# RWKV attention and an eight-expert MoE on one core: chunk loads cut into even and odd rows, two GpSimd products swapped, two weight loads moved by some steps

## The chip, the core and the metric

The kernel runs on one NeuronCore of a Trainium2 chip. The metric is device time in microseconds (us) of one launch. The kernel before has three timed runs of 278.13, 279.83 and 283.46 us; their median, 279.83 us, is what the changed kernel is held against.

## The reference

Two stages in float32. Attention, for 4 batches, 8 heads, 768 tokens and 48 channels a head, is a linear recurrence:

```
for t in range(S):
    y[t]  = r[t] @ (state + outer(u * k[t], v[t]))
    state = w[t][:, None] * state + outer(k[t], v[t])
```

The MoE takes the 3072 rows of 384 channels that come out: a row is computed only where `x @ w_skip > 0`; its expert is the argmax of `x @ w_gate` over 8; then `x + p * (relu(x @ w1[e]) @ w2[e])` with p the softmax weight of that expert. Other rows pass through.

## The kernel before, in words

**Attention.** The sequence is cut into 24 chunks of 128 tokens (6 for each batch, lines 56 to 58). A chunk lies on 128 partitions, two groups of four heads, as one tile `wrk` with three column ranges: w (up to `R_OFF`), r (up to `K_OFF`) and k (up to `V_OFF`). Three `wrk` buffers rotate, so chunk i + 3 can be loaded once GpSimd has read chunk i for the last time. For a chunk, VectorE runs two scans over w: `q` (line 308) and, after a small reciprocal (line 323), `rh` (line 330). GpSimd forms three products of 128 x 512: `rk` = r k (line 317, needs the chunk alone), `kq` = k q (line 325, needs the scan `q`) and `rp` = r rh (line 334, needs the scan `rh`). TensorE multiplies `kq` and `rp` into `psA` (scores, line 358), `rk` into `psY` (line 377), transposes `kq` (line 348), and after VectorE has masked `psA` (line 364, two halves `asb`) and scaled `psY` (line 381) it forms the outputs (lines 409 and 413), which ScalarE copies out as `xT` (line 418) and which are turned back on TensorE (line 425), copied by ScalarE and stored.

**Order of the work.** It is written out by hand: a loop over steps s from -2 to 24. Step s prepares chunk s + 2 (scans on VectorE, products on GpSimd), scores chunk s + 1, finishes chunk s and stores chunk s - 1. Each engine runs its own instructions in this order. SyncE (SP) issues nearly all DMAs, also in this order: the load of chunk s + 4, the turned v `vt` (two DMAs, line 157) and v (line 177) of chunk s + 3, the store of chunk s - 1 (line 435), and in some steps one third of a weight tile (line 86, 512 KB). In the compiled program an SP DMA also waits until the SP DMA eight places before it has landed, since they share eight semaphores in turn.

**Weights.** `load_weights(e, q)` brings 1.5 MB, the w1 (q = 0) or w2 (q = 1) of expert e, in three thirds, one a step. Steps 5 to 7 load w2 of expert 0 into buffer r1; steps 16 to 18 load w1 of expert 1 into the same buffer, steps 19 to 21 load w1 of expert 0 into r0. The w2 of expert 0 is split into a high and a low part as it lies in r1 (ScalarE line 108, GpSimd line 109, one slice a step); the first slice of expert 1's w1 is split from step 18 on.

**Router.** After chunks 10, 18 and 24 a generator `router` is advanced between the attention's instructions. It marks token places: `hot` (on GpSimd line 538, on ScalarE lines 541 and 542, on VectorE line 536), and it splits gate weights: `gds` and `vals` on GpSimd (lines 582 and 586), `factors` on ScalarE (line 595), which VectorE reads behind the next scan `q`.

**MoE.** From the last step on TensorE runs the experts back to back: line 135 (w1 of expert 0 straight from r0), 671, then 901 to 903 and 927 to 929 for the experts 1 to 7. Rows are gathered and scattered by GpSimd's indirect DMAs (lines 446, 622, 838).

Of the kernel before, what the change touches and what calls it, by code (L numbers as in the profile page):

```python
# [43 lines left out]
V_OFF = K_OFF + NP * P  # L44
# [13 lines left out]
def rwkv_moe_kernel(ctx, tc, wrk, wrk0, vN, uP, wgs, wgp, w12, cst, out):  # L58
    nc = tc.nc
# [59 lines left out]
    def drain(g):  # L119
        for _ in g:  # L120
            pass
# [20 lines left out]
    with tc.tile_pool(name="att", bufs=2) as att, \  # L142
# [7 lines left out]
        def half(g, n_=HP):  # L150
            return slice(HP * g, HP * g + n_)
# [7 lines left out]
        def load_turned(i):  # L159
            for o in range(2):  # L160
                load_vt(nc.sync, vt_sb[i % (NBUF + 1)], i, o)

        cuts = {i: ((0, R_OFF), (R_OFF, V_OFF)) for i in range(5)}

        def load_chunk(i):
            b, c = seq[i]
            rows = wrk.rearrange("b c g d n -> (b c g d) n")
            at = 2 * D * chunk[i]
            t = wrk_sb[i % NBUF]
            to, at = (t, at - KO) if 0 < chunk[i] < n - 1 else (t[KO:LO], at)  # L170
            for c0, c1 in cuts.get(i, ((0, V_OFF),)):
                yield nc.sync.dma_start(to[:, c0:c1], rows[at:at + to.shape[0], c0:c1])

        def load_v(i):
            b, c = seq[i]
            v_sb[i] = att.tile([P, H, D], F32, tag="v", name=f"v{i}", bufs=4)
            nc.sync.dma_start(v_sb[i], vN[b, c])
# [114 lines left out]
        def mark_some(k=2):  # L292
            for _ in range(min(k, len(marks))):
                marks.popleft()()
# [5 lines left out]
        def prep_scan(i):  # L300
            wk = work[i] = {}
            t = wrk_sb[i % NBUF]
            n_ = NP * CW
            a3 = lambda z: z.rearrange("p (a j) -> p a j", a=NP)
            wk["w"] = t
            wk["r"], wk["k"] = a3(t[:, R_OFF:K_OFF]), a3(t[:, K_OFF:V_OFF])
            q = wk["q"] = att.tile([P, NP, CW], F32, tag="q", name=f"q{i}", bufs=2)
            nc.vector.tensor_tensor_scan(  # L308
                q.rearrange("p a j -> p (a j)")[:, ::-1], t[:, 1:1 + n_][:, ::-1],
                ones_at[:, 1:1 + n_][:, ::-1], 0.0, op0=ALU.mult, op1=ALU.max)  # L310
            rk = wk["rk"] = att.tile([P, NP, P], F32, tag="rk", name=f"rk{i}")
            if i > 1:
                bonus_keys(i)

        def bonus_keys(i):
            t = wrk_sb[i % NBUF]
            nc.gpsimd.tensor_tensor(work[i]["rk"].rearrange("p a j -> p (a j)"),  # L317
                                    t[:, R_OFF:K_OFF], t[:, K_OFF:V_OFF], op=ALU.mult)

        def prep_keys(i):  # L320
            wk = work[i]
            heads = wk["w"][:, 0:NP * CW].rearrange("p (a j) -> p a j", a=NP)
            nc.vector.reciprocal(heads[:, :, 0:1], wk["q"][:, :, 0:1])
            kq = wk["kq"] = att.tile([P, NP, P], F32, tag="kq", name=f"kq{i}")
            nc.gpsimd.tensor_tensor(kq, wk["k"], wk["q"][:, :, 1:1 + P], op=ALU.mult)  # L325

        def prep_reads(i):
            wk = work[i]
            rh = wk["rh"] = att.tile([P, NP, CW], F32, tag="rh", name=f"rh{i}", bufs=2)
            nc.vector.tensor_tensor_scan(  # L330
                rh.rearrange("p a j -> p (a j)"), wk["w"][:, 0:NP * CW], reads_at[:, :NP * CW],
                rowsk, op0=ALU.mult, op1=ALU.max)
            rp = wk["rp"] = att.tile([P, NP, P], F32, tag="rp", name=f"rp{i}", bufs=3)
            nc.gpsimd.tensor_tensor(rp, wk["r"], rh[:, :, :P], op=ALU.mult)  # L334
            if i < 2:
                bonus_keys(i)
# [339 lines left out]
        def fill(k, w=512):  # L676
            psw = ps1.tile([P, 512], F32, tag="psT", name="psw", bufs=2)
            for _ in range(k):
                nc.tensor.matmul(psw[:, :w], warm[:, :P], warm[:, :w], start=True, stop=True)

        with tc.manual_schedule():
            setup()
            fill(FILL0)
            parts = [(4, 0, i) for i in range(6, 12)] + [(15, 1, 0)] + [(19, 1, i) for i in range(1, 6)]
            for s in range(-2, n + 1):
                on = lambda i: 0 <= i < n
                if s == -2:
                    z = wgp[half(0), :2]
                    z = bass.AP(z.tensor, z.offset,
                                [z.ap[0], [(HP * NP + 2) * XW, 2], [1, 2 * XW]])  # L690
                    nc.sync.dma_start(wgp_sb[half(0)].rearrange("p g s x -> p g (s x)"), z)
                    for g in range(2):
                        at = 2 * (g ^ 1)
                        nc.sync.dma_start(wgp_sb[half(1), g, :, 2 * D:],
                                          wgp[half(g), at:at + 2, 2 * D:])
                if 3 <= s + 4 < n:
                    chunk_parts = load_chunk(s + 4)
                    if s + 4 in cuts:
                        next(chunk_parts)
                        load_v(s + 2)  # L700
                    drain(chunk_parts)
                if on(s + 3) and s + 3 >= 1:
                    load_turned(s + 3)
                    if s + 5 not in cuts:
                        load_v(s + 3)
                if s == 1:
                    nc.sync.dma_start(c_sb[:, C_IOTA:], cst[:, C_IOTA:])
                if s == LATE:
                    nc.sync.dma_start(wgs_sb, wgs)
                if on(s - 1):  # L710
                    store(s - 1)
                marked = len(marks)
                if pace[0] == 1:
                    mark_some()
                for i0, m in GROUPS:
                    if i0 + m == s:
                        pace[0] = 1 if i0 + m < LATE else 2
                        later.append(router(i0, m))
                        if i0 + m == LATE:
                            later.append(early())  # L720
                if on(s):
                    update(s)
                if on(s + 2):
                    prep_scan(s + 2)
                drip(pace[0])
                if on(s):
                    outputs(s)
                if on(s + 2):
                    prep_keys(s + 2)
                    drip(pace[0])  # L730
                    prep_reads(s + 2)
                while low_parts:
                    low_parts.pop()()
                if on(s):
                    evict(s)
                    carry(s)
                if on(s + 1):
                    scores(s + 1)
                    bonus_sums(s + 1)
                    rows_of_keys(s + 1)  # L740
                    if s == -1:
                        fill(2)
                        fill(3, 8)
                    flush()
                    mask(s + 1, 0)
                    mask(s + 1, 1)
                    bonus(s + 1)
                    drip(3 * pace[0])
                if on(s + 2):
                    prep_check(s + 2)  # L750
                if s == n - 1:
                    early_tokens(0)
                if on(s):
                    rows_out(s)
                flush(False)
                if pace[0] > 1:
                    mark_some(4)
                if s in (1, 2, 3):
                    nc.scalar.copy(*((trib, tri), (identb, ident),
                                     (iota, c_sb[:, C_IOTA:C_IOTA + 2 * P]))[s - 1])  # L760
                if s == 4:
                    nc.scalar.copy(desc[:, 0], c_sb[:, C_DESC:C_DESC + E])
                    nc.scalar.copy(toks_ps[:, :GROUPS[-1][1], :, 0], tok[:, GROUPS[-1][0]:])
                k = s + 1 - W_AT
                for eq, k0 in (((0, 1), 2), ((1, 0), 13), ((0, 0), 16)):
                    if k == k0:
                        gens[eq] = load_weights(*eq)
                    if k0 <= k < k0 + 3:
                        next(gens[eq])
                for _ in range(1 if s < 22 else 2):  # L770
                    if parts and k >= parts[0][0] and (not marked or s == 15):
                        split_high(*parts.pop(0)[1:])
# [346 lines left out]
```

## Time and profile before

| what | value |
|---|---|
| median of three runs | 279.83 us |
| the profiled execution: its time, and its span from first to last instruction | 279.76 us, 277.9 us |
| TensorE busy | 264.4 us (95%) |
| VectorE busy | 211.9 us (76%) |
| ScalarE, GpSimd busy | 157.1 us (57%), 146.6 us (53%) |
| DMA | 64.33 MB, mean 231 GB/s |
| attention, from the first scores to the first expert's matmul | 7.6 to 131.6 us |

Busy shares are means over unlike stages: the attention uses all engines and the DMA queues, the MoE mostly TensorE. A row of the timeline begins with start and duration in us; what stands in brackets is the idle time of the engine just before the row and what ended it.

### The profile page before, as it was taken

To read this page: it belongs to the slowest core of one execution; us is meant where nothing else is said; L and a number is where in the kernel's file an instruction comes from. 1 tells how busy PE (TensorE), PEld (TensorE's weight loads), DVE (VectorE), ACT (ScalarE), POOL (GpSimd) and SP (SyncE) were. 2 spreads that over 40 slices of the span, in tenths; PEclk is the share of its full clock that TensorE was granted. 3 is DMA by queue.
4 is the path that set the end of the run, shared out by engine and by line. 5 is a ranking of instruction groups with operands and counts; after the bars stand their busy time and mean duration, and the time that the engine had idled before them with its cause. 6 is when DMAs were issued, how large, how long until landed. Compare 5 with 4: busy or idle time off the path is not lost.

```text
span 277.9 us, 8937 instructions
## 1 busy us (share of the span) xinstructions
PE 264.4 (95%) x3599; PEld 244.0 (88%) x3600; DVE 211.9 (76%) x396; ACT 157.1 (57%) x456; POOL 146.6 (53%) x141
## 2 busy tenths in 40 slices
PE   8899799998999999899999999999999999999992
PEld 3688688887888888787999999999999999999992
DVE  7989789999999999972748597957859488594310
ACT  4365556775788857767326482926729276391300
POOL 6888677798999997984656636011030110201111
PEclk9999999999999999999999999999999999999998
DMA  7999999999877999961078997765662656700001
GB/s 244 279 300 326 322 331 366 374 333 312 270 229 253 319 351 344 267 233 61 28 227 302 337 310 255 240 229 225 225 248 81 235 212 226 266 14 28 9 5 42
DMA packets 26402, 64.33 MB, mean 231 GB/s; under 512 B 4062, under 2 KB 15380, under 8 KB 26352
## 3 DMA queue, kind: packets, MB, share of 16 engines
q1 hardware_dynamic: 24176, 58.37, 63.2%
q0 software_dynamic: 2048, 5.30, 6.0%
q8 instruction: 30, 0.49, 0.7%
q14 instruction: 20, 0.16, 0.2%
q10 hardware_dynamic: 128, 0.00, 0.0%
HBM read 56.61 MB, written 7.67 MB: 231 GB/s over the span
## 4 chain that ended last, share of the span: by engine, by line
PE 71%; DMA 8%; issue 6%; DVE 5%; POOL 4%; ACT 4%; SPq 0%; POOLq 0%; DVEq 0%
PE psO L927 7%; PE psO L929 7%; PE psO L928 6%; PE psH L901 6%; PE psH L902 6%; PE psH L903 6%; PE psY L409 6%; DMA wrk<-wrk 5%; PE psH L135 4%; PE psX L425 4%; PE psA L358 4%; PE psY L413 3%; PE psT L348 3%; PE psY L377 2%; DMA r<-w 2%
## 5 line engine op out<-in xcount | busy, mean ns | idle before, releaser
L838 POOL DMA_INDIRECT out<-fin,ids x16 | 16.9, 1054 | 95.2 <-DVE fin L936 89.2
L908 ACT ACTIVATE hh<-psH 128x240 fp32r<-128x240 f32 (+1 forms) x60 | 22.4, 374 | 54.4 <-PE psH L903 47.4
L901 PE MATMUL psH<-xTh,w1h 128*128 128x240 f32 x168 | 46.3, 276 | 0.0
L902 PE MATMUL psH<-xTl,w1h 128*128 128x240 f32 x168 | 46.3, 276 | 0.0
L903 PE MATMUL psH<-xTh,w1l 128*128 128x240 f32 x168 | 46.1, 274 | 0.0
L927 PE MATMUL psO<-w2h,hh 128*128 128x384 f32 (+1 forms) x120 | 40.9, 341 | 0.0
L929 PE MATMUL psO<-w2h,hl 128*128 128x384 f32 (+1 forms) x120 | 40.3, 335 | 0.0
L928 PE MATMUL psO<-w2l,hh 128*128 128x384 f32 (+1 forms) x120 | 40.2, 335 | 0.0
L364 DVE TENSOR_TENSOR asb<-psA,c_sb 128x512 f32<-128x512 f32 x48 | 30.6, 679 | 5.4 <-PE psA L358 5.3
L913 DVE SCALAR_TENSOR_TENSOR hl<-psH,hh 128x240 fp32r<-128x240 f32 (+1 forms) x60 | 24.2, 403 | 12.3 <-ACT hh L908 7.3
L317 POOL TENSOR_TENSOR rk<-wrk 128x512 f32<-128x512 f32 x24 | 30.7, 1278 | 4.2 <-DMA wrk<-wrk 1.6
L330 DVE TENSOR_TENSOR_SCAN rh<-wrk,rowsk,pss 128x520 f32<-128x520 f32 x24 | 31.1, 1297 | 2.3
L325 POOL TENSOR_TENSOR kq<-wrk,q 128x512 f32<-128x512 f32 x24 | 28.3, 1181 | 6.9 <-DVE q L308 4.9
L901 PEld LDWEIGHTS psH<-xTh,w1h 128*128 128x128 f32 x168 | 31.7, 189 | 0.1
L903 PEld LDWEIGHTS psH<-xTh,w1l 128*128 128x128 f32 x168 | 31.8, 189 | 0.0
L902 PEld LDWEIGHTS psH<-xTl,w1h 128*128 128x128 f32 x168 | 31.7, 189 | 0.0
L334 POOL TENSOR_TENSOR rp<-wrk,rh 128x512 f32<-128x512 f32 x24 | 28.4, 1182 | 5.4 <-DVE rh L330 4.1
L308 DVE TENSOR_TENSOR_SCAN q<-wrk,pss 128x520 f32<-128x520 f32 x24 | 29.5, 1229 | 0.6 <-ACT pss L595 0.4
L409 PE MATMUL psY<-asb,v 128*48 128x128 f32 x384 | 26.9, 275 | 2.6 <-DVE psY L381 2.5
L91 DVE TENSOR_TENSOR w2l<-r,w2h 128x512 fp32r<-128x512 f32 x42 | 27.8, 687 | 1.7 <-ACT w2h L90 1.6
L418 ACT COPY xT<-psY 128x512 f32<-128x512 f32 x24 | 14.1, 588 | 25.6 <-PE psY L413 20.6
L936 DVE SCALAR_TENSOR_TENSOR fin<-psO,gates,xg 128x384 f32<-128x384 f32 (+1 forms) x15 | 9.3, 618 | 25.0 <-PE psO L929 23.2
(159 smaller groups left out, 605.8 us busy)
## 6 DMA issues: line engine op xcount, KB each, us to landing
r<-w SPq DMA_DIRECT2D x48, 512.0 KB, 5.6
wrk<-wrk SPq DMA_DIRECT2D x17, 772.5 KB, 7.1
vt<-wrk SPq DMA_DIRECT2D x48, 96.0 KB, 5.8
v<-vN SPq DMA_DIRECT2D x24, 192.0 KB, 4.9
out<-x SPq DMA_DIRECT2D x24, 192.0 KB, 5.0
wrk<-wrk SPq DMA_DIRECT2D x5, 512.0 KB
wrk<-wrk SPq DMA_DIRECT2D x5, 260.5 KB
wrk<-wrk SPq DMA_DIRECT2D x2, 579.4 KB
```

The source lines that it names most:

```text
L308: nc.vector.tensor_tensor_scan(q.rearrange("p a j -> p (a j)")[:, ::-1], t[:, 1:1 + n_][:, ::-1], ones_at[:, 1:1 + n_][:, ::-1], 0.0, op0= ...
L317: nc.gpsimd.tensor_tensor(work[i]["rk"].rearrange("p a j -> p (a j)"), t[:, R_OFF:K_OFF], t[:, K_OFF:V_OFF], op=ALU.mult)
L330: nc.vector.tensor_tensor_scan(rh.rearrange("p a j -> p (a j)"), wk["w"][:, 0:NP * CW], reads_at[:, :NP * CW], rowsk, op0=ALU.mult, op1=AL ...
L334: nc.gpsimd.tensor_tensor(rp, wk["r"], rh[:, :, :P], op=ALU.mult)
L364: nc.vector.tensor_tensor(s, psa[g], tri.rearrange("p (o j) -> p o j", o=1).to_broadcast([P, NP, P]), op=ALU.mult)
L409: nc.tensor.matmul(y_at(a, g), v[:, 2 * a + g], wk["asb"][g][:, a], start=False, stop=True, skip_group_check=True)
L901: nc.tensor.matmul(ps, w1h[:, o:o + P], xTh[:, kc], start=(kc == 0), stop=False)
L902: nc.tensor.matmul(ps, w1h[:, o:o + P], xTl[:, kc], start=False, stop=False)
L903: nc.tensor.matmul(ps, w1l[:, o:o + P], xTh[:, kc], start=False, stop=(kc == KC - 1))
L927: nc.tensor.matmul(po, h[j, fc][0], w2h[:, o], start=(fc == 0), stop=False)
L928: nc.tensor.matmul(po, h[j, fc][0], w2l[:, o], start=False, stop=False)
L929: nc.tensor.matmul(po, h[j, fc][1], w2h[:, o], start=False, stop=(fc == FC - 1))
```

## The change

Three edits. The load of a chunk from 5 on, one DMA over its rows before, becomes two, one for its even and one for its odd rows (chunks 0 to 4 stay cut by columns). GpSimd's `rk` of chunks from 2 on is issued behind `kq` and ahead of `rp`, where it was issued ahead of `kq`. The thirds of expert 1's w1 are issued in steps 13 to 15 (k = 10 to 12, where s = k + 3) in place of 16 to 18, those of expert 0's w1 in steps 20 to 22 in place of 19 to 21.

```diff
-            for c0, c1 in cuts.get(i, ((0, V_OFF),)):
-                yield nc.sync.dma_start(to[:, c0:c1], rows[at:at + to.shape[0], c0:c1])
+            m = to.shape[0]
+            if i in cuts:
+                for c0, c1 in cuts[i]:
+                    yield nc.sync.dma_start(to[:, c0:c1], rows[at:at + m, c0:c1])
+            else:
+                for o in range(2):
+                    yield nc.sync.dma_start(to[o:m:2], rows[at + o:at + m:2, :V_OFF])
...
             rk = wk["rk"] = att.tile([P, NP, P], F32, tag="rk", name=f"rk{i}")
-            if i > 1:
-                bonus_keys(i)
...
             nc.gpsimd.tensor_tensor(kq, wk["k"], wk["q"][:, :, 1:1 + P], op=ALU.mult)
+            if i > 1:
+                bonus_keys(i)
...
-                for eq, k0 in (((0, 1), 2), ((1, 0), 13), ((0, 0), 16)):
+                for eq, k0 in (((0, 1), 2), ((1, 0), 10), ((0, 0), 17)):
```

The instructions of TensorE, VectorE and ScalarE keep their order. On GpSimd the three products of a chunk change places. Chunks 15 and 16, before (`w2l` is the low part of a weight slice; line numbers of the changed kernel are 3 to 5 higher):

```order
L109 TENSOR_TENSOR w2l_0_990<-r_01_805,w2h_0_989 128x512
L586 TENSOR_TENSOR vals_1371<-gds_1420,vals_1371 128x10
L538 TENSOR_SCALAR hot_0_1489<-iota,rall 128x256
L317 TENSOR_TENSOR rk_1505<-wrk_88 128x512
L325 TENSOR_TENSOR kq_1524<-wrk_88,q_1503 128x512
L334 TENSOR_TENSOR rp_1528<-wrk_88,rh_1526 128x512
```

and of the change:

```order
L109 TENSOR_TENSOR w2l_0_997<-r_01_810,w2h_0_996 128x512
L591 TENSOR_TENSOR vals_1382<-gds_1432,vals_1382 128x10
L543 TENSOR_SCALAR hot_0_1502<-iota,rall 128x256
L328 TENSOR_TENSOR kq_1536<-wrk_88,q_1516 128x512
L320 TENSOR_TENSOR rk_1518<-wrk_88 128x512
L339 TENSOR_TENSOR rp_1541<-wrk_88,rh_1539 128x512
```

The product `rk`, which waits for no scan, now stands between the two that do. On GpSimd at chunk 22, where the router's second round runs, before:

```order
L109 TENSOR_TENSOR w1l_1_2091<-r_10_1875,w1h_1_2090 128x512
L538 TENSOR_SCALAR hot_0_2207<-iota,rall 128x256
L538 TENSOR_SCALAR hot_2_2213<-iota,rall 128x256
L317 TENSOR_TENSOR rk_2239<-wrk_89 128x512
L582 TENSOR_TENSOR gds_2241<-gall,vals_2191 128x8
L325 TENSOR_TENSOR kq_2260<-wrk_89,q_2237 128x512
L334 TENSOR_TENSOR rp_2264<-wrk_89,rh_2262 128x512
L586 TENSOR_TENSOR vals_2191<-gds_2241,vals_2191 128x8
```

and of the change:

```order
L109 TENSOR_TENSOR w1l_1_2109<-r_10_1595,w1h_1_2108 128x512
L543 TENSOR_SCALAR hot_0_2226<-iota,rall 128x256
L543 TENSOR_SCALAR hot_2_2232<-iota,rall 128x256
L587 TENSOR_TENSOR gds_2257<-gall,vals_2210 128x8
L328 TENSOR_TENSOR kq_2276<-wrk_89,q_2254 128x512
L320 TENSOR_TENSOR rk_2256<-wrk_89 128x512
L339 TENSOR_TENSOR rp_2281<-wrk_89,rh_2279 128x512
L591 TENSOR_TENSOR vals_2210<-gds_2257,vals_2210 128x8
```

The same eight instructions stand ahead of and behind `rp`; only `rk` has moved. On SP, from the store of step 13 to that of step 14, with the semaphores each waits for, of the change (before, the row of `r_10` was not here, and the two rows of `wrk_88` were one):

```order
L440 DMA out<-x_1499 128x384 [waits DMAHW5_49,Activation_49]
L86 DMA r_10_1595<-w 128x1024 [waits DMAHW6_49,Pool_49]
L177 DMA wrk_88<-wrk 64x1545 [waits DMAHW7_49,DVE_49]
L177 DMA wrk_88<-wrk 64x1545 [waits DMAHW0_49]
L157 DMA vt_92<-wrk 48x2x256 [waits DMAHW1_49]
L157 DMA vt_92<-wrk 48x2x256 [waits DMAHW2_49]
L182 DMA v_1601<-vN 128x384 [waits DMAHW3_49,PE_49]
L440 DMA out<-x_1604 128x384 [waits DMAHW4_49,Activation_49]
L86 DMA r_10_1595<-w 128x1024 [waits DMAHW5_49]
```

The first third of expert 1's w1 now waits for GpSimd (`Pool`), which has to be through with the weights that lie in the same buffer, and chunk 18's load stands behind it. A step with a third of weights has seven SP DMAs where it had six, one without has six where it had five.

## Rows read from the trace of the kernel before

**Rows 1.** Windows: stretch, length; busy us (instructions) by engine; TensorE clock; DMA share; GB/s.

```profile
28.00:66.00 38.00, 35.41 (x764) 30.90 (x755) 34.35 (x49) 24.78 (x89) 29.49 (x26) 1.00 1.04 346
...
92.00:131.00 39.00, 36.56 (x780) 31.21 (x776) 32.08 (x59) 27.22 (x92) 32.08 (x33) 1.00 0.84 266
131.00:262.00 131.00, 130.99 (x1007) 130.19 (x1007) 93.37 (x201) 70.38 (x163) 35.25 (x33) 1.00 0.57 196
```

**Rows 2.** Timeline of GpSimd, chunk 10: start, us, instruction, idle before and its end.

```profile
52.50 1.18 POOL L325 TENSOR_TENSOR kq<-wrk,q 128x512 f32<-128x512 f32 x1 [0.75 <-DVE q L308]
54.05 1.18 POOL L334 TENSOR_TENSOR rp<-wrk,rh 128x512 f32<-128x512 f32 x1 [0.37 <-DVE rh L330]
```

**Rows 3.** Timeline of GpSimd, chunks 13 to 16.

```profile
68.38 1.18 POOL L325 TENSOR_TENSOR kq<-wrk,q 128x512 f32<-128x512 f32 x1 [0.19 <-DVE q L308]
...
72.38 1.30 POOL L317 TENSOR_TENSOR rk<-wrk 128x512 f32<-128x512 f32 x1
73.63 1.19 POOL L325 TENSOR_TENSOR kq<-wrk,q 128x512 f32<-128x512 f32 x1
74.76 0.22 POOL L582 TENSOR_TENSOR gds<-gall,vals 128x10 f32<-128x10 f32 x1
75.05 1.20 POOL L334 TENSOR_TENSOR rp<-wrk,rh 128x512 f32<-128x512 f32 x1
...
82.02 1.27 POOL L109 TENSOR_TENSOR w2l<-r,w2h 128x512 fp32r<-128x512 f32 x1
...
86.53 1.19 POOL L334 TENSOR_TENSOR rp<-wrk,rh 128x512 f32<-128x512 f32 x1
```

**Rows 4.** Timeline of VectorE (scan q of chunk 14) and TensorE (scores of chunks 15, 16).

```profile
72.13 1.23 DVE L308 TENSOR_TENSOR_SCAN q<-wrk,pss 128x520 f32<-128x520 f32 x1
...
83.17 1.05 PE L358 MATMUL psA<-rp,kq 64*64 64x128 f32 x32
...
88.05 1.05 PE L358 MATMUL psA<-rp,kq 64*64 64x128 f32 x32
```

**Rows 5.** Timeline of GpSimd, chunks 21 and 22.

```profile
109.74 1.18 POOL L334 TENSOR_TENSOR rp<-wrk,rh 128x512 f32<-128x512 f32 x1 [0.37 <-DVE rh L330]
110.88 1.27 POOL L109 TENSOR_TENSOR w1l<-r,w1h 128x512 fp32r<-128x512 f32 x1
112.27 1.82 POOL L538 TENSOR_SCALAR hot<-iota,rall 128x256 bf16<-128x256 bf16 x2
117.72 0.22 POOL L586 TENSOR_TENSOR vals<-gds,vals 128x8 bf16<-128x8 f32 x1
```

**Rows 6.** Timeline of ScalarE and VectorE: factors, and the scan q of chunk 23.

```profile
117.97 0.20 ACT L595 CAST pss<-vals 128x40 f32<-128x40 bf16 x1 [0.61 <-POOL vals L586]
118.20 1.24 DVE L308 TENSOR_TENSOR_SCAN q<-wrk,pss 128x520 f32<-128x520 f32 x1 [0.35 <-ACT pss L595]
```

**Rows 7.** Chunk loads: issue at 41.45, and all issued from 70 to 93.

```profile
DMA to landing us min/median/max: 6.6/6.6/6.6
...
DMA to landing us min/median/max: 4.5/4.5/4.5
```

**Rows 8.** Timeline of VectorE: the scans q of chunks 10 and 18.

```profile
51.13 1.23 DVE L308 TENSOR_TENSOR_SCAN q<-wrk,pss 128x520 f32<-128x520 f32 x1
...
90.96 1.23 DVE L308 TENSOR_TENSOR_SCAN q<-wrk,pss 128x520 f32<-128x520 f32 x1
```

**Rows 9.** Timeline of TensorE: a pause inside line 377, and the first expert matmul.

```profile
30.65 0.42 PE L377 MATMUL psY<-rk,ubk_sb 64*48 64x128 f32 x3 [1.60 <-issue]
...
131.57 0.63 PE L135 MATMUL psH<-xT,r 128*128 128x128 f32 x4
```

**Rows 10.** Timeline of SP: chunk 18's load, and the store of step 22.

```profile
82.08 0.33 SPq L172 DMA_DIRECT2D wrk<-wrk  x1
...
123.56 0.34 SPq L435 DMA_DIRECT2D out<-x  x1
```

**Rows 11.** DMA issues by line: count, KB each, median us from issue to landing.

```profile
r<-w SPq DMA_DIRECT2D x48, 512.0 KB, 5.6
```

## The prediction

> **What bounds the kernel now.** I began with the busy time of each engine by stretch. From 131 us to 262 us TensorE is busy 130.99 of 131 us at the full clock [rows 1]: the experts run back to back, so whatever shifts the end of the attention shifts the end of the kernel by as much, and nothing behind 131 us gives it back. The edits all lie in the attention, ahead of that. There three engines run close together: in the 38 us from 28 us TensorE is busy 35.41, VectorE 34.35 and GpSimd 29.49 us, while the DMA engines stand at a share of 1.04; from 92 to 131 us it is 36.56, 32.08 and 32.08 us with a DMA share of 0.84 [rows 1]. So the question is not which engine is busiest but where TensorE has to wait. A step takes 4.88 us when it does not wait: scores start at 83.17 and 88.05 us [rows 4].
>
> Next I read GpSimd's timeline in a step where it keeps up. For chunk 10 it waits 0.75 us for the scan `q`, forms `kq`, waits 0.37 us for the scan `rh` and forms `rp` [rows 2]. In that order `rk`, which needs no scan, runs ahead of both, in time in which GpSimd would have waited for `q`. From chunk 14 to chunk 16 the timeline has no such waits [rows 3]: weight splits and the router's `hot` fill GpSimd, and each instruction follows the last.
>
> Last I compared the landing of chunk loads with their use. Chunk 10 is issued at 41.45 us, lands 6.6 us later, at 48.05 us [rows 7], and is scanned at 51.13 us [rows 8]: 3.1 us to spare under the full DMA load. Chunk 18 is issued at 82.08 us [rows 10], lands 4.5 us later where weights do not load [rows 7], at 86.6 us, and is scanned at 90.96 us [rows 8]: 4.4 us to spare. Loads are late for nobody in these steps.
>
> **Part 1: `rk` behind `kq`.** Nothing is added, so where GpSimd is never idle the end of `rp` stays where it is. Where it does wait, `rk` leaves a free place and takes one that is free for 0.37 us only. `rk` costs 1.25 us from its start to the next (72.38 to 73.63 us [rows 3]), so `rp` comes 1.25 - 0.37 = 0.88 us later [rows 2, 5]. The scores need `rp`, and so does the next load into that buffer. In most steps nobody notices: `rp` of chunk 10 ends at 54.05 + 1.18 = 55.2 us [rows 2], and its scores stand a step later in the order. Two places notice.
>
> *Chunks 14 to 16.* `kq` of chunk 13 starts at 68.38 us in either order. Then come `kq`, `rk`, `rp` and a weight split, 1.18 + 1.30 + 1.20 + 1.27 = 4.95 us [rows 3], some 0.1 us less as starts overlap, so GpSimd is free by about 73.3 us. The scan of chunk 14 ends at 72.13 + 1.23 = 73.36 us [rows 4], and `kq` follows at about 73.45 us. Before, the block of `rk`, `kq`, `gds`, `rp` began at 72.38 us and lost 0.07 us ahead of `rp` (74.76 + 0.22 to 75.05 us [rows 3]). The block now begins 1.07 us later and loses nothing, so `rp` is 1.0 us later, and with no idle time behind it that lag reaches `rp` of chunk 16: it ended at 86.53 + 1.19 = 87.72 us [rows 3] and will end at 88.72 us. TensorE began those scores at 88.05 us [rows 4]. It waits **0.67 us**. VectorE masks what TensorE delivers, and from there to 118 us it hardly idles, so the shift stays.
>
> *Chunks 21 to 23.* `rp` of chunk 21 waited 0.37 us for its scan [rows 5], so it is again 0.88 us late. The weight split that began at 110.88 us begins at 111.76 and ends near 113.0 us; the two `hot` behind it began at 112.27 us [rows 5], so they are 0.75 us late. The rest of GpSimd's work up to `vals` (117.72 us) is the same set of instructions without a gap. ScalarE's factors wait for `vals`, and VectorE's scan `q` of chunk 23 waits for the factors (0.35 us idle ahead of 118.20 us [rows 6]); masks and outputs of chunk 22 stand behind that scan. They are **0.75 us** later. This comes on top of the first shift, since both sides of it move along.
>
> Bounds: nothing, if VectorE's slack takes up the first and the scan's wait the second; 0.88 us more than the sum, if a third place notices. I take 0.67 + 0.75 = 1.42 us.
>
> **Part 2: even and odd rows.** The same rows and bytes, one more DMA a step. Its issue costs SP about 0.33 us (a chunk issue takes that [rows 10]), and SP does no other work. No engine waits for a load from chunk 7 on, so an earlier landing gains nothing and one up to 3 us later costs nothing. The Trainium skill ("DMA: Bandwidth & Descriptors", section Rules for kernel authors) advises against two transfers to disjoint parts of the partitions, since both spread over the same 16 engines and come one behind the other; by that rule too the halves land no sooner, and the sum would be the same. I take 0. The bounds come from a stall of TensorE by itself: at 30.65 us it resumes after 1.60 us in which it waited for nothing the profile shows [rows 9], in a stretch where DMA is full. If that is its program code arriving late behind large loads, smaller loads may end it: -1.60 us. Another such stall would be +1.60 us.
>
> **Part 3: weights.** 1.5 MB of expert 1's w1 leave steps 16 to 18, where loads had time to spare, for steps 13 to 15, which hold no other weights. Nobody reads them before step 18. On SP the first third now waits for the split that ran from 82.02 to 83.29 us [rows 3], 1.0 us later by part 1, so chunk 18 goes out near 84.9 us in place of 82.08. With 4.5 us to land and an estimate of 1.5 us for the 512 KB ahead of it at the 346 GB/s of the full stretch [rows 1], it is there by 90.9 us; its scan, also 0.67 us later, comes at 91.6 us. That is covered with 0.7 us to spare, and is the thinnest cover here. Expert 0's last third goes out behind the store at 123.56 us [rows 10], 1.4 us later by part 1, near 125.4 us, and lands a median 5.6 us after issue [rows 11], at 131.0 us; the first expert matmul was at 131.57 us [rows 9] and will be at 133. I take 0 for both; gone cover would cost the difference, under 1 us each.
>
> **Sum.** 279.76 us of the profiled execution + 1.42 = **281.2 us**. That execution lies 0.07 us under the median of 279.83 us, which I leave out.
>
> **Rivals.** (a) *The stall at 30 us goes*, and part 1 costs what I say: 281.2 - 1.6 = 279.6 us. For it: the stretch has a DMA share of 1.04, and the stall fell between two chunk loads. Against it: the same share holds up to 62 us without another such pause. The skill (same page, section Queues, rings and completion order) says that an engine of the DMA turns from one queue to another only between packets; by that rule a code fetch waits less behind half a load, which gives this same time. No row here shows where a packet ends.
>
> (b) *Faster*: the stall goes, and part 1 is hidden because the DMA load from 92 to 120 us, without weights, lets GpSimd and VectorE wait less: 279.76 - 1.6 = 278.2 us. Against it: I found no wait for a load there.
>
> (c) *Slower, by SP's turn of eight semaphores.* In a step with weights SP has seven DMAs, so a chunk's second half waits until the first half of the chunk before has landed. If that takes longer than a step of 4.88 us, three such steps run late by three times the difference. Whole loads took 6.6 us under full load [rows 7]; if a half takes 7.0 us, that is 3 x 2.1 = 6.4 us, of which 3.1 us are spare: 281.2 + 3.3 = 284.5 us. It decides from 4.88 + 3.1 / 3 = 5.9 us on. Against it: half a chunk is 386 KB, about 1.1 us less to move than the whole at 346 GB/s, so 5.5 us.
>
> (d) *The change does nothing that can be seen*: the lag of part 1 is taken up: 279.8 us.
>
> **Numbers.** My forecast 0.45, (a) 0.22, (b) 0.13, (c) 0.13, (d) 0.07. The range of 277.6 to 284.5 us takes in all five with a little under (b) for the spread of the runs, and leaves out the worse half of (c) and what I have not thought of. More than 2% from the median, about what a measurement of this kernel can tell from no change, is under 274.2 or over 285.4 us. No case reaches the first; I give it 0.04. The second takes the tail of (c), 0.07. Within: 0.89.
>
> **What would show it.** In the profile of the changed kernel GpSimd should run `kq`, `rk`, `rp` without a gap between them and `rp` should end about 0.9 us later behind its scan; scores of chunk 16 should wait for `rp`; the scan `q` of chunk 23 should wait longer for the factors; the first expert matmul should start at 133 us, or at 131.4 us without the stall. It is wrong if a scan waits for a chunk load, above all chunk 18's, if SP's issues fall behind in steps 5 to 7, or if the first expert matmul starts under 131 us with the stall still there.

## The result, and the profile after

The changed kernel took 283.05 us (median of 22 runs, 279.41 to 289.25), the kernel before on the same chip 280.13 us: a ratio of 1.010, 95% interval 1.0070 to 1.0131. It is about 2.8 us slower, where 1.4 were forecast. The profiled execution took 283.21 us with a span of 281.4 us.

The windows of the changed kernel, which answer to [rows 1] (stretch, length; busy us and instructions by engine; TensorE clock; DMA share; GB/s):

```profile
28.00:66.00 38.00, 35.54 (x772) 31.16 (x766) 35.21 (x50) 25.40 (x89) 31.40 (x27) 1.00 0.99 333
92.00:131.00 39.00, 35.78 (x775) 30.71 (x774) 32.29 (x59) 26.55 (x89) 31.23 (x32) 1.00 0.79 263
131.00:262.00 131.00, 128.83 (x992) 127.53 (x985) 92.38 (x197) 70.07 (x162) 37.35 (x34) 1.00 0.57 197
```

The clock is the same. What differs most is the last row: TensorE, which before was busy for 130.99 of 131 us, is now idle for 2.17 us, 1.94 of it behind 133 us, where the experts run. So there are two losses to find, one up to 131 us and one behind it. TensorE's timeline after names the places (start, us, instruction, idle time before and what ended it):

```profile
65.92 1.08 PE L414 MATMUL psY<-asb,v 128*48 128x128 f32 x16 [1.96 <-DVE psY L386]
...
88.33 0.97 PE L363 MATMUL psA<-rp,kq 64*64 64x128 f32 x29 [0.51 <-POOL rp L339]
...
133.00 0.74 PE L135 MATMUL psH<-xT,r 128*128 128x128 f32 x5
...
161.77 0.38 PE L906 MATMUL psH<-xTh,w1h 128*128 128x240 f32 x1 [1.93 <-DVE hl L918]
```

The pause at 30.65 us [rows 9] has no counterpart. The first row, the outputs of chunk 12, waits 1.96 us for VectorE (0.86 before). The wait for `rp` at the scores of chunk 16 is there, where before there was none [rows 4]. The first expert matmul starts at 133.00 us instead of 131.57 [rows 9]. VectorE's timeline after, the scans `q` of chunks 11, 12 and 23:

```profile
55.16 1.24 DVE L313 TENSOR_TENSOR_SCAN q<-wrk,pss 128x520 f32<-128x520 f32 x1 [0.82 <-DMA wrk<-wrk]
60.46 1.24 DVE L313 TENSOR_TENSOR_SCAN q<-wrk,pss 128x520 f32<-128x520 f32 x1 [0.66 <-DMA wrk<-wrk]
...
119.63 1.24 DVE L313 TENSOR_TENSOR_SCAN q<-wrk,pss 128x520 f32<-128x520 f32 x1 [1.49 <-ACT pss L600]
```

Two scans wait for their chunk load, which none did before, and the one of chunk 23 waits 1.49 us for the factors instead of 0.35 [rows 6]. Taking the start of each chunk's scores after, less its start before, the attention's shift builds up so:

| up to the scores of chunk | shift, us | step | what stands there after |
|---|---|---|---|
| 5 to 10 | -1.76 | -1.76 | no pause at 30 us |
| 12 | -0.41 | +1.35 | scans of chunks 11 and 12 wait for loads |
| 16 | +0.28 | +0.69 | scores wait for `rp` |
| 20 | +0.77 | +0.49 | scans of chunks 19 and 20 start 0.66 us behind the last packets of their loads (those of 11 and 12: 0.67 and 0.53) |
| 23, and the first expert matmul | +1.43 | +0.66 | scan of chunk 23 waits for the factors |

Behind it come 2.07 us more: from the first expert matmul to the end the kernel before took 146.34 us (the span of 277.9 us less 131.57), the changed one 148.41. GpSimd for chunk 10, to set against [rows 2]:

```profile
50.73 1.18 POOL L328 TENSOR_TENSOR kq<-wrk,q 128x512 f32<-128x512 f32 x1 [1.17 <-DVE q L313]
51.87 1.27 POOL L320 TENSOR_TENSOR rk<-wrk 128x512 f32<-128x512 f32 x1
53.11 1.17 POOL L339 TENSOR_TENSOR rp<-wrk,rh 128x512 f32<-128x512 f32 x1
```

`rk` now lies between them, `kq` waits 1.17 us for the scan instead of 0.75, and `rp` ends 4.91 us behind the start of the scan `q` (49.37 to 54.28) instead of 4.10 (51.13 to 55.23). And ScalarE at the hidden layer of expert 1, where the loss behind 131 us begins:

```profile
156.63 0.37 ACT L913 ACTIVATE hh<-psH 128x240 fp32r<-128x240 f32 x1 [3.85 <-PE psH L908]
156.90 0.61 ACT L90 CAST w1h<-r 128x512 fp32r<-128x512 f32 x1
160.91 0.37 ACT L913 ACTIVATE hh<-psH 128x240 fp32r<-128x240 f32 x1 [3.40 <-PE psH L908]
```

The second activation could have followed the cast at 157.5 us: the last of its matmuls began at 156.53. It came 3.40 us later, and TensorE, which had run on to the fifth group, had no free tile for the next (`psH` rotates through four). The releaser named is the one inferred last; TensorE's rows show no pause between 154.6 and 159.6 us that would have held it.

### The profile page after: what moved, and what is told of

Its sections match the earlier page's. It is cut to its first block, busy times and chain, and to the rows that moved or that the text cites. A ratio compares the mean times of both kernels' runs of the same rounds, so it can differ in the third digit from the quotient of the medians.

```text
span 281.4 us, 8970 instructions
## 1 busy us (share of the span) xinstructions
PE 265.5 (94%) x3599; PEld 244.3 (87%) x3600; DVE 211.8 (75%) x396; ACT 157.6 (56%) x456; POOL 146.8 (52%) x141
## 4 chain that ended last, share of the span: by engine, by line
PE 49%; issue 4%; ACT 2%; POOL 1%; DVE 1%; POOLq 0%; DVEq 0%
PE psH L908 7%; PE psO L932 7%; PE psO L934 6%; PE psO L933 6%; PE psH L906 6%; PE psH L907 6%; PE psH L135 4%; PE psX L836 2%; PE psO L676 2%; PE psX L430 1%; PE psY L414 1%; POOL out L843 1%; ACT xT L423 1%; PE psY L418 1%; PE psY L382 0%
## 5 line engine op out<-in xcount | busy, mean ns | idle before, releaser
L843 POOL DMA_INDIRECT out<-fin,ids x16 | 17.8, 1110 | 96.1 <-DVE fin L941 90.6
```

## The experiments

Every run was timed against the kernel before on the same chip. The kernel before itself took a median 280.3 us beside e1 to e4, 279.2 beside e5 to e8 and 279.3 beside e9 to e12, so times of different groups are compared by the ratio. One table for all; "attention" is the start of the first expert matmul, "rest" from there to the end, "issue" TensorE's idle time without a releaser from 15 to 131 us. "Gap" is taken at the very end: the time from the start of GpSimd's last instruction ahead of its final two semaphore instructions to the start of the first of these. All but the ratio come from one profiled execution each.

| run | ratio to before, 95% | attention | rest | issue | GpSimd instructions | gap |
|---|---|---|---|---|---|---|
| before | | 131.57 | 146.34 | 1.60 | 260 | 0.09 |
| changed | 1.0100 (1.0070 to 1.0131) | 133.00 | 148.41 | 0.43 | 259 | 0.09 |
| e1 changed, again | 1.0114 (1.0070 to 1.0158) | 135.11 | 147.20 | 0 | 259 | 0.09 |
| e2 halves alone | 1.0071 (1.0018 to 1.0125) | 131.94 | 147.48 | 0 | 274 | 1.21 |
| e3 GpSimd's order alone | 1.0084 (1.0035 to 1.0132) | 135.18 | 146.07 | 3.16 | 245 | 0.09 |
| e4 weights alone | 1.0011 (0.9967 to 1.0055) | 132.35 | 146.46 | 2.91 | 260 | 0.09 |
| e5 halves, chunks 5 and 6 | 0.9986 (0.9946 to 1.0026) | 132.89 | 146.06 | 1.90 | 262 | 0.09 |
| e6 halves, from chunk 7 | 1.0079 (1.0040 to 1.0117) | 131.57 | 147.25 | 2.22 | 272 | 1.14 |
| e7 changed, whole loads | 1.0078 (1.0037 to 1.0119) | 135.27 | 146.08 | 1.55 | 245 | 0.09 |
| e8 changed, `rk` first | 1.0072 (1.0040 to 1.0104) | 131.42 | 147.22 | 0.69 | 272 | 1.21 |
| e9 before, 13 memsets more | 1.0054 (1.0015 to 1.0093) | 131.24 | 147.41 | 0.81 | 273 | 1.36 |
| e10 as e6, 24 memsets more | 1.0082 (1.0054 to 1.0111) | 133.93 | 146.22 | 0.59 | 296 | 0.09 |
| e11 changed, 16 copies more | 1.0114 (1.0058 to 1.0170) | 131.82 | 146.09 | 0.55 | 259 | 0.09 |
| e12 changed, four buffers | 1.0168 (1.0122 to 1.0213) | 134.41 | 146.08 | 0.62 | 259 | 0.09 |

**e1.** The changed kernel unedited.

> The changed kernel once more. The comparison of the two traces gives its loss as a sum of places: -1.75 us near 30 us (the 1.60 us idle of TensorE is gone), +1.34 at chunks 11 and 12 (scans wait for chunk loads), +0.68 at chunk 16 and +0.66 at chunk 23 (r k late), up to +0.45 at chunks 18 and 19 (scans wait for their loads), and +2.0 us in the experts (ScalarE stood from 157.4 to 160.9 us). Theory S (the last term belongs to the change): ratio 1.01 again, and a second profile shows ScalarE standing 3 us or more at the hidden layer of expert 2 again. Rival R (it strikes one execution or another): the second profile shows it elsewhere or not at all, with the last attention matmul again near 131.5 to 133 us.

The loss was there again, 1.0114. ScalarE stood at the same activation, though 1.26 us and not 3, and the rest took 147.20 us. The attention ended at 135.11 us, 2.1 later than in the first profile of the same program: a single profile can't price a part to a microsecond here. Of the 2.1 us, 1.15 had built up by the scores of chunk 14, where the scans of chunks 10 to 12 waited for loads, and 0.92 between those of chunks 17 and 20. There it was chunk 18's load that came late, the one whose cover the prediction called the thinnest:

```profile
93.41 1.24 DVE L313 TENSOR_TENSOR_SCAN q<-wrk,pss 128x520 f32<-128x520 f32 x1 [0.85 <-DMA wrk<-wrk]
```

ScalarE's standing is less sharp than in the first profile: shorter waits of up to 1.3 us stand at other activations of the same layer in e3 and e4 too, whose rest took 146.07 and 146.46 us.

**e2, the halves alone.**

```diff
-            for c0, c1 in cuts.get(i, ((0, V_OFF),)):
-                yield nc.sync.dma_start(to[:, c0:c1], rows[at:at + to.shape[0], c0:c1])
...
+                for o in range(2):
+                    yield nc.sync.dma_start(to[o:m:2], rows[at + o:at + m:2, :V_OFF])
```

> The kernel before with only the loads from chunk 5 on as even and odd rows. Theory A (the places of the trace belong to the parts as the comparison puts them): the 1.60 us idle near 30 us is gone and the scans of chunks 11 and 12 wait some 1.3 us for their loads: -0.3 to -0.5 us, 279.4 to 279.9 against 279.8 to 280.1 of before. Theory B (what the prediction said): 0, the idle near 30 us stays. Rival C (SP's turn of eight semaphores): 284, scans wait in most steps from 5 to 12.

Right about the places, wrong in the sum. The pause was gone and the scans of three chunks waited 2.1 us in all for loads, so the attention ended 0.37 us later than before. But the kernel was 0.7% slower, and its profile lost 1.14 us behind the attention, where none of the three theories had looked.

**e3, GpSimd's order alone.**

```diff
             rk = wk["rk"] = att.tile([P, NP, P], F32, tag="rk", name=f"rk{i}")
-            if i > 1:
-                bonus_keys(i)
...
             nc.gpsimd.tensor_tensor(kq, wk["k"], wk["q"][:, :, 1:1 + P], op=ALU.mult)
+            if i > 1:
+                bonus_keys(i)
```

> The kernel before with only GpSimd's k q ahead of r k. Theory A and B: +1.4 us (0.67 at the scores of chunk 16, 0.75 at the scan of chunk 23), 281.2 to 281.6, and the 1.60 us idle near 30 us stays. Rival D (the idle near 30 us hangs on GpSimd's order, not on the loads): that idle is gone and the sum is -0.3 us.

The ratio allows 1.0 to 3.7 us, and 1.4 lies in it. Both places show in its profile, TensorE first and VectorE behind:

```profile
31.69 0.42 PE L377 MATMUL psY<-rk,ubk_sb 64*48 64x128 f32 x3 [2.27 <-issue]
...
90.99 0.97 PE L358 MATMUL psA<-rp,kq 64*64 64x128 f32 x29 [0.55 <-POOL rp L334]
...
121.81 1.24 DVE L308 TENSOR_TENSOR_SCAN q<-wrk,pss 128x520 f32<-128x520 f32 x1 [1.49 <-ACT pss L595]
```

The scores of chunk 16 lost 0.73 us against a step of 4.88 and the scan of chunk 23 waited 1.49 us, as in the changed kernel. The pause near 30 us stayed, so rival D falls. The profile's loss of 3.6 us at the end of the attention is larger than the two places: 1.6 us of it is more idle time without a releaser (3.16 against 1.60).

**e4, the weights alone.**

```diff
-                for eq, k0 in (((0, 1), 2), ((1, 0), 13), ((0, 0), 16)):
+                for eq, k0 in (((0, 1), 2), ((1, 0), 10), ((0, 0), 17)):
```

> The kernel before with only the weights' steps moved. Theory B (prediction): 0, chunk 18's load lands 0.7 us before its scan. Theory A: 0 to +0.45 us, the load of chunk 18 or 19 lands behind the end of the scan's other wait, and the scan waits. Rival E (the experts' loss hangs on which weights come when): +2 us in the experts, 282.

No difference that 12 runs can measure, but the profile shows the thin cover give way, two chunks later than the one I had named. Chunk 18's last semaphore update came at 90.63 us, 0.4 ahead of its scan (its last packet at 89.25). The last packet of chunk 20, issued at 92.48 us, landed 8.3 us later, and its scan waited (100.91 us before):

```profile
101.68 1.24 DVE L308 TENSOR_TENSOR_SCAN q<-wrk,pss 128x520 f32<-128x520 f32 x1 [0.62 <-DMA wrk<-wrk]
```

The shift of 0.77 us stays to the end of the attention (132.35 us). Rival E falls: the rest took 146.46 us.

**e5 and e6, halves for some chunks.** e5 loads only chunks 5 and 6 as halves, e6 only those from 7 on:

```diff
+            elif not (i in (5, 6)):
+                yield nc.sync.dma_start(to[:, :V_OFF], rows[at:at + m, :V_OFF])
```

> The kernel before with only the loads of chunks 5 and 6 as even and odd rows. Theory A (the split moves chunk 6's load from 22.1 to 23.8 us and so lets TensorE's instructions come 1 to 3 us sooner; its price lies in the loads of chunks 9 to 12): the idle without releaser near 30 us is gone (1.60, 1.40 and 2.27 us with whole loads, at most 0.43 with halves), no scan from chunk 9 on waits for its load, and the attention ends 1.2 to 1.7 us sooner: 278.4 to 279. Rival F (what is won there is lost at the next place that is late whatever the loads are): the idle is gone, the scans of chunks 10 to 13 wait for whole loads too, and the time is 280 to 281. Rival G (the idle has to do with the halves from chunk 7 on): it stays, 280.

> The kernel before with only the loads from chunk 7 on as even and odd rows. Theory A: the idle near 30 us stays at 1.4 to 2.3 us, and since the scans then come 1.7 us later, the loads of chunks 9 to 12 land in time or up to 0.5 us late: 0 to +0.5 us, 280 to 280.7. Rival H (each half load is late by itself): scans of chunks 9 to 12 wait 1.3 us, 281.5 to 282.

e5 gained nothing that can be measured. TensorE paused 0.90 us at 30.99 us and 0.83 us at 50.43 us, both without a releaser: shorter, and one more elsewhere. That fits none of the three in full: the pause is not gone, and no scan from chunk 9 on waited for its load. In e6 the pause was 1.81 us and the attention ended at 131.57 us, to the hundredth where it ended before. So halves from chunk 7 on cost the attention nothing, no scan from chunk 9 on waited for a load, and rival H falls. Yet e6 was 0.8% slower, and its rest took 0.91 us more. What the halves cost had to lie at the end.

**e7 and e8, one part of the change undone.** e7 has the whole loads again (the lines of e2 turned back), e8 has `rk` first again (those of e3).

> The changed kernel with whole loads again (GpSimd's order and the weights' steps as changed). Theory A: the idle near 30 us is back (+1.6), the waits of chunks 11 and 12 are gone (-1.3), chunk 16 and 23 still pay 1.4: near the changed kernel, 282 to 283.3. Rival I (the parts add as e2 to e4 measured, +2.0, +2.0 and -0.3 us by the medians): 281.8, over a microsecond under the changed kernel.

> The changed kernel with r k ahead of k q again (halves and the weights' steps as changed). Theory A: the 0.68 us at chunk 16 and the 0.66 us at chunk 23 are gone, the waits for the loads of chunks 9 to 12 stay: 1.3 us under the changed kernel, 281.6 to 282. Rival J (r k's place costs nothing once scans wait for loads): 283.

Taken by the ratio, e7 is 2.2 us over the kernel before (1.0 to 3.3) and e8 2.0 (1.1 to 2.9). Rival I and theory A of e7 meant some 1.7 and 1.9 to 3.2 us over it, theory A and rival J of e8 1.5 to 1.9 and 2.9, so these times decide neither. Nor do they show whether the parts add: e2 to e4 sum to 1.7% and all three parts together measure 1.0 to 1.1%, and the intervals leave that difference open. The profile of e7 shows that whole loads can be late as well. Its scans of chunks 10 to 12:

```profile
52.00 1.24 DVE L308 TENSOR_TENSOR_SCAN q<-wrk,pss 128x520 f32<-128x520 f32 x1 [0.52 <-DMA wrk<-wrk]
57.09 1.24 DVE L308 TENSOR_TENSOR_SCAN q<-wrk,pss 128x520 f32<-128x520 f32 x1 [0.45 <-DMA wrk<-wrk]
62.19 1.24 DVE L308 TENSOR_TENSOR_SCAN q<-wrk,pss 128x520 f32<-128x520 f32 x1 [0.35 <-DMA wrk<-wrk]
```

Chunk 10 went out at 43.23 us (41.30 in e4, the same loads with `rk` first) and its last packet landed at 51.40 (47.88). The place of `rk` is not what held it: from 38 to 62 us SP waited 8.1 us for earlier transfers and not once for `rp`, and in e3, with whole loads and `rk` behind `kq` too, none of these scans waited. In e8 the scores of chunk 16 waited for nothing, and the scan of chunk 23 waited 0.35 us, as before.

**e9 and e10, GpSimd's number of instructions.** In the profiles of e2, e6 and e8 GpSimd stood 1.14 to 1.21 us ahead of the last semaphore of the program, elsewhere 0.09 us. A load in two halves has two semaphores, and a product that waits for both has a further waiting instruction: the halves bring GpSimd's waiting instructions from 76 to 90 and the whole from 260 to 274. `rk` behind `kq`, which has waited for the same load, takes them to 61 and the whole to 245; with both it is 259. None of the other engines holds GpSimd there: in e9 the last semaphore that it waits for came at 276.88 us, ahead of its instruction at 277.10, and it went on at 278.46. e9 gives the kernel before 13 tiny instructions at its start and nothing else, e10 gives e6 24 of them:

```diff
             nc.gpsimd.memset(vt_sb[3], 0.0)
+            for _ in range(13):
+                nc.gpsimd.memset(idle, 0.0)
```

> The kernel before with 13 memsets of one column more on GpSimd ahead of its first product, where it stands idle from 3.3 to 4.9 us, and nothing else: 273 instructions on GpSimd instead of 260. Theory K (what the halves cost lies at the very end: with 272 or 274 instructions on GpSimd, as in e2, e6 and e8, it stands 1.14 to 1.21 us ahead of its last semaphore, with 245 to 262 only 0.09): that gap is there, the stretch from the last combining of an expert's output to the end is 6.1 to 6.5 us instead of 5.1, the rest as before, and the ratio is 1.004. Rival L (the gap belongs to the loads themselves): gap 0.09, ratio 1.000.

> e6 (halves from chunk 7 on) with 24 such memsets on GpSimd at the same place, which computes nothing more of use: 296 instructions on GpSimd. Theory K: the last semaphore is no longer the first of what GpSimd has to fetch, the gap is 0.09 us again, and the kernel is faster than e6 by 1 us with more work: ratio to the kernel before 1.000 to 1.004 instead of 1.0079. Rival L: gap 1.1 to 1.2, ratio 1.008.

The last transfer that GpSimd starts in each of four kernels, from its timeline; the tail is the span (277.9, 279.4, 278.7 and 280.2 us) less that start. Before:

```profile
273.73 0.95 POOL L838 DMA_INDIRECT out<-fin,ids  x1 [3.17 <-DVE fin L936]
```

e2:

```profile
273.83 0.95 POOL L843 DMA_INDIRECT out<-fin,ids  x1 [3.17 <-DVE fin L941]
```

e9:

```profile
273.14 0.95 POOL L841 DMA_INDIRECT out<-fin,ids  x1 [3.17 <-DVE fin L939]
```

e10 (with its memsets and the first product behind them):

```profile
3.25 3.70 POOL L258 MEMSET idle<- 128x1 f32 x24
7.00 1.17 POOL L335 TENSOR_TENSOR kq<-wrk,q 128x512 f32<-128x512 f32 x1
...
275.95 0.95 POOL L848 DMA_INDIRECT out<-fin,ids  x1 [3.17 <-DVE fin L946]
```

The tails are 4.2, 5.6, 5.5 and 4.2 us. Thirteen memsets lengthened the tail by 1.3 us, 270 us later, and made the kernel before 0.5% slower; 24 on top of e6's 272 instructions took the gap away. Theory K holds for the gap. e10's time missed, for a reason of its own: its memsets took 3.70 us and so outlasted the idle time from 3.3 to 4.9 us that was to hold them, the first `kq` began at 7.00 us instead of 5.02, and the attention ended 2.4 us later than in e6.

e9 shows one thing more. Its loads are whole, `rk` stands first and its weights are where they were, but its pauses were short, 0.36 and 0.45 us. The scores of chunk 5 started 0.98 us sooner than before, those of chunk 14 only 0.34, since the scans of chunks 11 and 12 came too soon for their loads. That of chunk 11:

```profile
55.37 1.24 DVE L311 TENSOR_TENSOR_SCAN q<-wrk,pss 128x520 f32<-128x520 f32 x1 [0.25 <-DMA wrk<-wrk]
```

**e11, ScalarE's number of instructions.**

```diff
+            for _ in range(16):
+                nc.scalar.copy(idle, warm[:, 0:1])
             eye = ident[half(1, D), HP:LO]
```

> The changed kernel with 16 copies of one column more on ScalarE near 4 us, where it waits for its first inputs. Theory M (ScalarE's standing before the second activation of expert 1's hidden layer, 3.40 us in the first profile of the changed kernel and 1.26 in the second, is a wait for instructions): 16 instructions more put the border elsewhere, it does not stand there, experts' part (first early matmul to the end) 146.0 to 146.5 us instead of 147.2 to 148.4, time 1 to 2 us under the changed kernel. Rival N (it hangs on the gathers or weights under way): it stands there again, 283.

In its profile ScalarE did not stand at the hidden layer of expert 1:

```profile
154.62 0.37 ACT L916 ACTIVATE hh<-psH 128x240 fp32r<-128x240 f32 x1 [3.12 <-PE psH L911]
154.89 0.61 ACT L90 CAST w1h<-r 128x512 fp32r<-128x512 f32 x1
155.64 0.37 ACT L916 ACTIVATE hh<-psH 128x240 fp32r<-128x240 f32 x1
```

The rest took 146.09 us, as theory M had it, but the ratio stayed at 1.0114. The profiled execution, 279.70 us, was the fastest of the six runs, whose median is 282.37. The same activation stood in both profiles of the changed kernel and in none of the others, e4, e7, e8 and e12 among them, whose ScalarE runs the same 552 instructions. That speaks against the number of instructions alone. Neither theory is shown.

**e12, four chunk buffers.**

```diff
-        NBUF = 3
+        NBUF = 4
```

> The changed kernel with four chunk buffers instead of three (a load no longer waits for r p of three chunks before). Theory P (the waits of the scans of chunks 10 to 12 and 18 to 20 for their loads, 1.3 and 0.45 us, come from loads that go out late: a buffer freed by a later r p, and the second half behind SP's eight semaphores): the first cause is gone, the loads go out earlier by up to 1 us and the waits shrink by half or more; 281.3 to 282.3. Rival Q (only the semaphores' turn holds them): the loads go out when they did, 283. Rival R (loads that go out sooner share the engines with the weights and land no sooner): 283.

Theory P falls. Chunk 10 went out at 42.32 us (41.64 in the changed kernel) and its scan waited for nothing, but those of chunks 11 and 12 did:

```profile
55.38 1.24 DVE L313 TENSOR_TENSOR_SCAN q<-wrk,pss 128x520 f32<-128x520 f32 x1 [0.22 <-DMA wrk<-wrk]
60.97 1.24 DVE L313 TENSOR_TENSOR_SCAN q<-wrk,pss 128x520 f32<-128x520 f32 x1 [0.93 <-DMA wrk<-wrk]
```

The buffer was not what held the loads. The ratio, 1.0168, is above the changed kernel's 1.0100 and 1.0114, though the intervals touch; why was not tried.

## Why the prediction was right, and where not

The time lay in the range and within 2% of before. The sum was half of what was measured: 1.42 us against 2.0 to 3.7.

**Part 1** holds. The next table takes the start of TensorE's weight loads for each chunk's scores, less that of the kernel before, and gives by how much this shift grew (us) in three stretches of each profile:

| profiles | scores of chunk 15 to 17 | 17 to 20 | 22 to 23 |
|---|---|---|---|
| `rk` behind `kq`, weights moved: changed, e1, e7, e11, e12 | 0.65, 0.66, 0.66, 0.66, 0.65 | 0.49, 1.41, 1.00, 0.17, 1.33 | 0.66, 0.66, 0.68, 0.69, 0.69 |
| `rk` behind `kq`, weights not moved: e3 | 0.66 | 0.00 | 0.67 |
| `rk` first, weights moved: e4, e8 | 0.00, 0.00 | 0.71, 0.52 | -0.01, 0.00 |
| neither: e2, e5, e6, e9, e10 | 0.00 in each | 0.00 in each | -0.01 to 0.01 |

Both places appear wherever `rk` is behind `kq` and nowhere else, at 0.66 us (forecast 0.67) and 0.66 to 0.69 (forecast 0.75); the row of `rp` and the 1.49 us ahead of the scan of chunk 23 stand in e3 too. No third place follows from the order in these profiles. By time the order costs 1.0 to 3.7 us alone (e3), and 1.42 lies in it.

**Part 2** is a step that failed: "one up to 3 us later costs nothing... I take 0". By time the halves alone cost 0.5 to 3.5 us (e2). Three things came of the halves. The first is rival (a): with halves throughout, TensorE's idle time without a releaser was 0 to 0.69 us (the changed kernel, e1, e2, e8, e11, e12), with whole loads or halves for some chunks 0.59 to 3.16 us (the other eight), on average 0.38 against 1.84. That gain of some 1.5 us is a tendency and not a switch: e9, with whole loads, had 0.81, and no run tells why a pause comes. The second is that scans came to wait for loads. SP's timeline after, one load without a third of weights ahead of it and two with one (start, us):

```profile
33.04 1.13 SPq L177 DMA_DIRECT2D wrk<-wrk  x2
...
46.65 1.71 SPq L177 DMA_DIRECT2D wrk<-wrk  x2
...
52.68 1.85 SPq L177 DMA_DIRECT2D wrk<-wrk  x2
```

The pair of issues takes 0.6 to 0.7 us longer in the last two rows, as SP's second half waits its turn behind the first half of the chunk before. That is the wait that rival (c) names, but it did not make the halves late: from the first issue to the last semaphore update, the loads of chunks 9 to 12 took a mean of 7.6 us in the eight profiles that load them as halves and 7.7 us in the six that load them whole. What changed is when the scans came. Those of chunks 11 and 12 waited in every profile with at most 0.81 us of pauses, e9 with its whole loads among them, except e10, whose attention started later. They waited in e7 (1.55 us) and in none with pauses of 1.60 us or more. The slack I counted was in good part the pause itself: the seven profiles with short pauses that waited lost 0.6 to 2.3 us of their start again between the scores of chunks 5 and 14. At the scores of chunk 14 the six profiles with halves throughout stand between -1.33 and +0.74 us from the kernel before, the others between -0.34 and +2.35: up to there the halves cost the attention nothing that shows. The Trainium skill ("DMA: Bandwidth & Descriptors", section Rules for kernel authors) calls two transfers to disjoint partition halves not worth it, as they share the same engines; 7.6 against 7.7 us, no gain to speak of, agrees with it.

The third was in no rival, and it is where the halves cost: two semaphores for one load make further waiting instructions on whoever reads it, and GpSimd's count alone decides 1.1 to 1.4 us at the end (e9, e10). That it is the fetch of its last instructions is my reading and not shown. The instruction packets in the traces don't settle it: one starts 0.3 to 0.5 us ahead of the gap in e2, e6, e8 and e9, and one at the same place in the kernel before and the changed one, which have no gap. The Trainium skill ("Runtime: NRT & Kernel Launch", section Instruction fetch mechanics) says that engines fetch their program by DMA in blocks ahead of use and that crossing into the next one is mostly hidden; the gap, if it is that, was not. With `rk` behind `kq` GpSimd is back at 259 instructions, so the changed kernel takes the halves without this gap.

**Part 3** is the other step that failed, though 0 lies within what the times can measure (e4: -0.9 to +1.5 us). The table above shows 0.17 to 1.41 us lost between chunks 17 and 20 in all seven profiles with the moved weights and nothing in the others. The loads of chunks 18 to 20 share the DMA engines with expert 1's weights of steps 13 to 15. The cover named as the thinnest, chunk 18's, was forecast at 0.7 us; measured from the last semaphore update to the scan it was 0.4 us in e4 and 0.2 in the changed kernel (a scan that waits starts 0.1 to 0.2 us behind it), and in e1 the scan waited. The covers of chunks 19 and 20, which the prediction had not worked out, gave way in more profiles.

**"Nothing behind 131 us gives it back"** was true, but it hid that something there could be lost. The rest took 146.06 to 146.46 us in the eight kernels without gap and stand, 147.2 to 147.5 in the four with the gap, and 147.20 and 148.41 in the two profiles of the changed kernel. What makes ScalarE stand stays open, and how often it does.

So the excess over the sum is, in the two profiles of the changed kernel, 0.5 and 1.4 us at chunks 18 to 20 and 2.07 and 0.86 us behind the attention, with -0.41 and +0.74 us up to chunk 14. By time these terms are not told apart. Up to chunk 14 the 0 of part 2 came near by luck, since it had neither the gain nor the loss there.

That the first expert matmul started at 133.00 us, as forecast, is a coincidence: -1.76, +1.35 and +0.49 us, none of them in the sum, cancelled to 0.08, and in e1 they did not. Of the signs of being wrong that the prediction named, two came: scans waited for loads, chunk 18's among them in e1, and SP's issues fell behind. Of the rivals, (a) came true together with the waits of (c), which the chances had not allowed for. No version beat the kernel before: e5 (0.9946 to 1.0026) and e4 can't be told from it.

## What to carry to other kernels

Before a transfer is cut in two, count the instructions of every engine that waits for it, and look at the end of the kernel too: a further semaphore is a further instruction, and here where the program's last instructions fell cost more than the transfer. Slack that is measured while an unexplained pause stands earlier in the trace may belong to that pause; work the slack out again without it. One profile can't price a part of a microsecond, since the attention of one and the same program ended at 133.0 and 135.1 us in two of them, and a dozen timed runs leave a microsecond or more open. But the same place compared over the profiles of many versions, with the part and without it, can show a loss of 0.7 us.

## What the runs showed of the hardware

- GpSimd's last semaphore came 1.14 to 1.36 us after the instruction ahead of it in the programs with 272, 272, 273 and 274 instructions on it, and 0.09 us after it in those with 245 to 262 and 296.
- 24 memsets of one column into the same tile on GpSimd took 3.70 us (e10): 99 ns each, 157 ns from one start to the next. One of 512 columns takes 0.53 us.
- TensorE's pauses without a releaser near 30 us (0 to 2.27 us) come and go between executions and programs whose TensorE instructions are the same.
